# Two row tiles of a Fourier product taken by symmetry: rows turned through memory instead of multiplied

## The chip, the core and the metric

The kernel runs on one core of one Trainium2 chip. A core has five engines, each working through its own list of instructions in order: TensorE (PE, matrix products into PSUM), VectorE (DVE), ScalarE (ACT), GpSimd (POOL) and SyncE (SP, which here only issues DMAs). They wait for each other through semaphores. POOL can issue DMAs as well, and the indirect ones, whose row addresses come out of a table in SBUF, are issued there. The metric is device time in microseconds (us) of one execution; lower is better.

## The reference, cut to what matters

There are four batches of 768 positions and 8 heads of 64. First block-sparse causal attention is computed, whose heads side by side give `x`, 768 rows of 512. Then an FNet layer follows, and that is what the change touches:

```python
X = np.fft.fft(x, axis=1)               # over the 768 positions
X = np.fft.fft(X, axis=2)               # over the 512 columns
mixed = np.real(X).astype(np.float32)
u = x + mixed
mu, var = mean and variance of u over a row
un = (u - mu) / np.sqrt(var + 1e-06)
ch = np.maximum(un @ w_ch1, 0.0) @ w_ch2     # 512 -> 2048 -> 512
return (u + ch).astype(np.float32)
```

`x` is real, so the real part of its two-dimensional transform has a symmetry: row 768-k holds the same numbers as row k, with column 512-l in place of column l (indices modulo 768 and 512).

## The kernel before, in words

**One list orders all work.** `ORDER` (L114) is a long string of steps, each a short name and its indices. The loop at the end of the kernel function, under `tc.manual_schedule` (L842), calls the step's function for each, and the instructions are appended to the engines' lists in that order. No scheduler moves anything afterwards. A second string, `PLACES`, says for each PSUM tile which of four slots (`ps0` to `ps3`, two banks each) it takes. So a PE step that opens a new tile waits until the last reader of the slot's former tile is done.

**Attention** goes by pairs of heads, numbered 0 to 15, four to a batch. For pair P, `g`, `gt`, `gx`, `gl`, `gm` work out which key blocks are kept (PE, then DVE), `K` writes the mask rows (POOL, L473), `s:P,i` are the score products (PE), `e:P,i` the exponentials (ACT, `s_exp`, L516), `d:P,i` cuts the diagonal blocks (POOL, L522), `v` multiplies with the values (PE, L534), `x` divides and writes `x_b` (DVE). `kc`, `qs`, `kh`, `vc` bring keys, queries and values into place (ACT and POOL).

**The Fourier stage of batch b** folds `x` by its symmetries (`fs`, `fd`, `f` on DVE, `fc` on POOL), and multiplies over positions: `y:b,h,gg` (PE, L604) gives two PSUM tiles, h = 0 and 1, which `ty:b,h` brings to SBUF (ACT, `y_copy`, L617) and `tr:b,h` copies once more with the columns reversed (DVE, `y_turn`, L624). The second product, over columns, is `m:b,kp` (PE, `m_mm`, L636 and L637). Each call makes two of the six row tiles of 128 rows, with eight matmuls of 256 columns; the even and the odd columns of the result stand in separate halves. Row tiles 0, 1 and 2 read `ty`, row tiles 3, 4 and 5 read `tr`.

`u:b,kt` (DVE, `m_u`, L650) adds `x` to row tile kt and sums its rows, and reads the product straight from PSUM. `nm` (ACT, L658) makes the mean of it, `xu` (ACT, L664) writes the centred tile in half precision, `un` (SP, L679) is a DMA that transposes this tile into `unT`, and `bn` (DVE, L684 and L685) makes the variance.

**The two products with the weights** are `w:b,it` (PE, `w1_mm`, L719), which reads all of `unT` and makes one of 16 hidden tiles, `r` (ACT, L729, or DVE, L727) its ReLU, and `c:b,st,h` (PE, `w2_mm`, L744), which makes half of the sum over hidden tiles for row tile st: eight matmuls of 512 columns. `o` (DVE, L756) adds the result to `u`, and `od` (SP, L761) stores it. `nv` and `nr` work out the reciprocal deviation (DVE and POOL). The six `u` tiles of a batch live in three buffers of two tiles each, out of a pool of five; a buffer comes free when its `od` DMAs have landed.

The work of neighbouring batches is interleaved: while the Fourier stage of batch 3 goes its way through ACT, DVE and SP, PE works on `c` steps of batch 2.

Of the kernel before, what the change touches and what calls it, by code (L numbers as in the profile page):

```python
# [11 lines left out]
FP = mybir.dt.float32  # L12
# [7 lines left out]
S = 768  # L20
DM = 512
# [70 lines left out]
for _pieces in SC_TILES:  # L92
# [16 lines left out]
R3 = (1,)  # L109
W2_CUTS = (0, 256, 384, 512)  # L110
# [4 lines left out]
tq:0,0 qc:0,0 Lk:1 tk:0,0 ks:0,0 tk:0,1 ks:0,1 kc:0,1 tq:0,1 kh:0 kc:0,0 qc:0,1 qs:0 tk:1 ks:1 kh:1  # L115
g:0 gt:0 gx:0 gl:0,0 gl:0,1 gm:0 Lk:2 tk:2 Lq:1 tq:1 qc:1 qs:1 ks:2 kh:2 iz:0 iz:1 s:0,2 kc:1 e:0,2
s:0,5 e:0,5 g:1 gt:1 gx:1 gl:1,0 gl:1,1 gm:1 kc:2 s:0,4 e:0,4 s:0,3 s:0,0 e:0,0 e:0,3 Lq:3 Lq:2 tq:2
qc:2 qs:2 tq:3 qc:3 d:0,4 s:1,4 e:1,4 Lk:4 Lv:0 vc:0 d:0,3 d:0,2 d:0,0 d:0,5 s:0,1 e:0,1 d:0,1 g:2
gt:2 gx:2 gl:2,0 gl:2,1 gm:2 s:1,0 e:1,0 s:1,1 s:1,2 e:1,1 tk:4 ks:4 kh:4 Lk:3 tk:3 ks:3 kh:3 qs:3
d:1,4 e:1,2 d:1,2 kc:4 kc:3 v:0 x:0 s:1,3 e:1,3 d:1,3 Lq:4 tq:4 qc:4 fs:0,1 s:2,2 g:3 s:1,5 e:2,2  # L120
gt:3 gx:3 gl:3,0 gl:3,1 s:2,1 e:1,5 Lv:1 vc:1 qs:4 s:2,5 e:2,1 d:1,5 d:1,1 d:2,2 e:2,5 d:1,0 d:2,5
g:4 gt:4 s:2,0 e:2,0 gx:4 gm:3 Lk:5 tk:5 s:2,3 ks:5 s:2,4 d:2,1 kh:5 d:2,0 e:2,3 d:2,3 Lq:5 tq:5
qc:5 qs:5 gl:4,0 fs:0,0 gl:4,1 Lv:2 e:2,4 d:2,4 vc:2 kc:5 v:1 x:1 s:3,2 e:3,2 Lv:3 vc:3 s:3,4 g:5
gt:5 gx:5 gm:4 fs:1,0 gl:5,0 e:3,4 d:3,4 s:3,3 s:3,0 e:3,0 s:3,5 e:3,5 d:3,5 d:3,2 d:3,0 e:3,3 d:3,3
v:2 gl:5,1 x:2 fs:2,0 fs:2,1 gm:5 fs:1,1 fd:2,1 fd:2,0 s:3,1 e:3,1 d:3,1 W:1 s:4,1 e:4,1 s:4,2 s:4,3
e:4,3 e:4,2 v:3 x:3 fs:3,1 fs:3,0 fd:3,1 fd:3,0 f:0,1 fc:0 f:0,0 s:4,5 s:5,2 e:5,2 e:4,5 d:4,5 s:4,0
e:4,0 d:4,0 s:5,0 e:5,0 LT:0 Lq:6 Lk:6 s:5,1 tk:6 ks:6 e:5,1 d:4,2 d:5,2 d:4,3 s:4,4 e:4,4 d:5,1
y:0,0,0 y:0,0,1 ty:0,0 kc:6 f:0,2 f:0,3 y:0,1,0 y:0,1,1 ty:0,1 tr:0,0 tr:0,1 s:5,3 e:5,3 s:5,4 e:5,4
LF:0 m:0,0 u:0,0 nm:0,0,1 xu:0,0 u:0,1 nm:0,1,1 m:0,2 s:5,5 e:5,5 u:0,4 nm:0,4,1 xu:0,1 u:0,5
nm:0,5,1 m:0,1 u:0,2 u:0,3 xt:0,0 tq:6 qc:6 xt:0,1 un:0,0 W:0 Lv:4 vc:4 d:4,1 kh:6 d:4,4 d:5,0 v:4  # L130
xu:0,4 xt:0,4 nm:0,2,1 xu:0,5 xt:0,5 un:0,2 g:6 gt:6 xu:0,2 nm:0,3,1 xu:0,3 xt:0,2 xt:0,3 w:0,6,2
w:0,6,0 w:0,5,2 w:0,5,0 un:0,1 w:0,5,1 w:0,6,1 r:0,5 r:0,6 gx:6 gl:6,0 gl:6,1 gm:6 x:4 w:0,3 r:0,3
Lq:7 tq:7 Lk:8 tk:8 ks:8 fs:4,0 Lk:7 tk:7 ks:7 bn:0,0 bn:0,4 qs:6 s:6,3 e:6,3 s:6,2 s:6,4 e:6,4
s:6,1 e:6,2 e:6,1 w:0,4,2 w:0,4,1 w:0,4,0 w:0,2 r:0,4 r:0,2 kc:8 w:0,7,2 w:0,0 w:0,7,1 r:0,0 w:0,7,0
r:0,7 d:5,4 W:2 w:0,13 d:5,3 d:5,5 d:6,1 d:6,4 d:6,3 qs:7 s:6,5 e:6,5 Lv:5 s:6,0 kh:7 g:7 gt:7 gx:7
gl:7,0 gl:7,1 gm:7 e:6,0 bn:0,1 Lq:8 Lc:0 tq:8 Lq:9 w:0,14 r:0,14 r:0,13 w:0,15 w:0,12 r:0,15 kh:8
vc:5 v:5 x:5 K:7 d:6,2 qs:8 kc:7 r:0,12 s:7,2 e:7,2 d:7,2 w:0,11 r:0,11 g:8 gt:8 gx:8 gl:8,0 fs:5,1
fs:5,0 gl:8,1 gm:8 d:6,5 X:0 s:7,0 e:7,0 d:7,0 X:1 d:6,0 K:8 Lk:9 tk:9 ks:9 kh:9 tq:9 bn:0,5 bn:0,3
# [738 lines left out]
```

## Time and profile before

| | |
|---|---|
| median of 3 runs | 284.72 us (283.73 to 284.79) |
| profiled execution, its own time | 284.69 us |
| its span (first to last instruction) | 283.0 us |
| PE busy | 273.7 us, 97% of the span |
| DVE busy | 190.8 us, 67% |
| ACT busy | 166.3 us, 59% |
| POOL busy | 120.7 us, 43% |
| granted TensorE clock, mean | 0.999 |

The span is shorter than the execution's own time by 1.7 us, which lie around it. An engine's busy time is the union of its instructions' intervals. A matmul's interval in the profile is longer than the step at which the next one follows, so that a busy PE can hide gaps of about 0.1 us. For a sum, the step from one start to the next is what counts.

### The profile page before, as it was taken

How to read it: one execution, taken by the hardware profiler on the slowest of the kernel's cores; microseconds unless marked ns; L12 is line 12 of the kernel's file. 1: busy time of each engine (PE TensorE's matmuls, PEld its weight loads, DVE VectorE, ACT ScalarE, POOL GpSimd, SP SyncE). 2: the span in 40 equal slices, each digit the busy share in tenths (PEclk: the TensorE clock that was granted, in tenths of full speed). 3: DMA queues.
4: the chain of work that ended last, by engine and by line, in shares of the span. 5: the costliest groups of instructions: out<-in, count | busy, mean ns of one | idle time of the engine just before them, and what ended most of it. 6: DMA issues, size and time to landing. Idle time of an engine off the chain costs nothing.

```text
span 283.0 us, 6718 instructions
## 1 busy us (share of the span) xinstructions
PE 273.7 (97%) x2593; PEld 170.0 (60%) x2593; DVE 190.8 (67%) x570; ACT 166.3 (59%) x222; POOL 120.7 (43%) x313
## 2 busy tenths in 40 slices
PE   7799998999999999999999999999999999999995
PEld 3567676876656646565665574566576555665453
DVE  2789998998899797998988669550376443380032
ACT  3599899668787269886497634669641261343100
POOL 2157839306895658747546538701522000002000
PEclk9999999999999999999999999999999999999999
DMA  7999999996999999459795152610000042000044
GB/s 179 231 218 212 222 189 154 182 189 115 156 136 203 150 131 211 63 107 193 153 205 108 28 161 74 120 71 0 0 3 2 30 110 46 2 37 0 2 166 169
DMA packets 119152, 33.45 MB, mean 118 GB/s; under 512 B 110736, under 2 KB 115920, under 8 KB 119120
## 3 DMA queue, kind: packets, MB, share of 16 engines
q1 hardware_dynamic: 113712, 28.43, 50.7%
q0 software_dynamic: 3664, 4.19, 9.6%
q10 hardware_dynamic: 1744, 0.40, 0.7%
q8 instruction: 20, 0.33, 0.5%
q14 instruction: 12, 0.10, 0.1%
HBM read 28.55 MB, written 6.29 MB: 123 GB/s over the span
## 4 chain that ended last, share of the span: by engine, by line
PE 81%; DVE 7%; DMA 3%; ACT 3%; POOL 3%; issue 2%; ACTq 0%; POOLq 0%; DVEq 0%
PE c L744 28%; PE h L719 28%; PE sc L499 7%; PE av L534 6%; PE yp L604 3%; ACT pt L516 2%; PE mx L636 2%; DMA nat<-in_k_dram 2%; PE mx L637 2%; DMA nat<-in_q_dram 1%; PE c L737 1%; DVE kr L362 1%; PE g L424 1%; PE sc L494 1%; POOL qk L246 1%
## 5 line engine op out<-in xcount | busy, mean ns | idle before, releaser
L516 ACT ACTIVATE pt<-sc 128x1024 f16<-128x1024 f32 (+1 forms) x96 | 82.8, 926 | 25.7 <-PE sc L499 17.5
L719 PE MATMUL h<-unT,w 128*128 128x256 f16 (+1 forms) x528 | 87.2, 321 | 0.0
L744 PE MATMUL c<-w_sb,hT 128*128 128x512 f16 x368 | 83.8, 379 | 0.0
L719 PEld LDWEIGHTS <-w 128*128 128x128 f16 x528 | 50.8, 98 | 31.0 <-issue 0.3
L744 PEld LDWEIGHTS <-hT 128*128 128x128 f16 x368 | 35.6, 98 | 40.2 <-issue 0.5
L729 ACT ACTIVATE hT<-h 128x768 f16<-128x768 f32 x48 | 37.8, 811 | 34.9 <-PE h L719 34.9
L522 POOL TENSOR_SCALAR_AFFINE_SELECT pt<-pt 128x256 f16<-128x256 f16 x96 | 38.0, 421 | 35.3 <-ACT pt L516 34.8
L756 DVE SCALAR_TENSOR_TENSOR u<-c,rs,u 128x512 f32<-128x512 f32 (+2 forms) x26 | 17.6, 702 | 36.4 <-PE c L744 33.3
L727 DVE TENSOR_SCALAR hT<-h 128x768 f16<-128x768 f32 x16 | 15.1, 951 | 22.0 <-PE h L719 21.9
L246 POOL TENSOR_SCALAR_AFFINE_SELECT qk<-mt 32x160 f16<-32x160 f16 x72 | 23.6, 348 | 14.1 <-DVE mt L471 12.6
L246 POOL TENSOR_SCALAR_AFFINE_SELECT qk<-q 64x768 f16<-64x768 f32 (+1 forms) x25 | 20.8, 832 | 18.8 <-DVE q L398 7.4
L499 PE MATMUL sc<-qk 96*128 96x512 f16 (+3 forms) x144 | 26.7, 306 | 0.0
L534 PEld LDWEIGHTS <-pt 128*128 128x128 f16 x672 | 22.2, 97 | 2.3 <-issue 0.7
L534 PE MATMUL av<-v,pt 128*128 128x65 f16 x672 | 23.0, 193 | 0.3 <-POOL v L246 0.3
L243 POOL TENSOR_TENSOR t<-vr,rs 128x6 f32<-128x6 f32 x12 | 2.7, 225 | 41.0 <-DVE rs L695 40.2
L499 PEld LDWEIGHTS <-qk 96*128 96x128 f16 x144 | 12.9, 98 | 9.2 <-issue 0.8
L246 POOL TENSOR_SCALAR_AFFINE_SELECT v<-nat 128x768 f16<-128x768 f32 x16 | 14.7, 922 | 5.2 <-DMA nat<-in_v_dram 5.1
L650 DVE SCALAR_TENSOR_TENSOR u<-mx,x 128x512 f32<-128x512 f32 x24 | 15.3, 683 | 2.1 <-PE mx L637 1.9
L494 PE MATMUL sc<-qk 64*128 64x512 f16 (+3 forms) x112 | 14.8, 307 | 1.9 <-ACT pt L516 0.6
L664 ACT ACTIVATE x<-u,nm 128x512 f16<-128x512 f32 x24 | 16.1, 712 | 0.3
L684 DVE BATCH_NORM_STATS2 bst<-u 128x6 f32<-128x512 f32 x24 | 16.1, 672 | 0.0
L243 DVE TENSOR_TENSOR x<-av,rcp 128x768 f16<-128x768 f32 x16 | 15.3, 958 | 0.6
(106 smaller groups left out, 318.0 us busy)
## 6 DMA issues: line engine op xcount, KB each, us to landing
nat<-in_v_dram SPq DMA_DIRECT2D x16, 384.0 KB, 5.0
out_dram<-u SPq DMA_DIRECT2D x23, 256.0 KB, 2.5
nat<-in_k_dram SPq DMA_DIRECT2D x38, 96.0 KB, 3.7
nat<-in_q_dram SPq DMA_DIRECT2D x38, 96.0 KB, 3.8
nat<-in_k_dram SPq DMA_DIRECT2D x12, 192.0 KB, 4.5
nat<-in_q_dram SPq DMA_DIRECT2D x12, 192.0 KB, 5.1
w_sb<-in_moe_w_ch_dram POOLq DMA_DIRECT2D x2, 1024.0 KB, 11.6
w<-in_moe_w_ch_dram POOLq DMA_DIRECT2D x2, 768.0 KB, 8.1
```

What stands on the lines that cost most here:

```text
L243: (eng or nc.vector).tensor_tensor(out=out, in0=in0, in1=in1, op=op)
L246: nc.gpsimd.affine_select(out=out, in_=in_, pattern=[[0, i] for i in n], base=0, channel_multiplier=0, compare_op=ALU.is_ge, fill=0.0)
L494: nc.tensor.matmul(ps[:, e, co:co + q1 - q0], qk[hs[e], 1, XW(P), 128 * jt:128 * jt + 128], qk[hs[e], 0, XW(P), q0:q1], start=(co == 0), s ...
L499: nc.tensor.matmul(ps[:, e, co:co + q1 - q0], qk[0:96, e, 1, 128 * jt:128 * jt + 128], qk[0:96, e, 0, q0:q1], start=True, stop=True)
L516: nc.scalar.activation(out=d["pt"][:, o:o + 2 * n].rearrange("p (e c) -> p e c", e=2), in_=d["sc", i][:, :, 0:n], func=AF.Exp, scale=0.125)
L522: nc.gpsimd.affine_select(out=dg, in_=dg, pattern=[[0, 2], [1, 128]], base=0, channel_multiplier=-1, compare_op=ALU.is_ge, fill=0.0)
L534: nc.tensor.matmul(av[:, e, 66 * st:66 * st + 65], pt[:, co:co + 128], vv[:, e, jt, 0:65], start=(cnt == 0), stop=(cnt == 20))
L664: nc.scalar.activation(out=x_t[b][:, kt, :], in_=u_t[b, kp][:, k2, :], func=AF.Identity, scale=0.0625, bias=u_t[b, kp, "m"][:, k2:k2 + 1])
L719: nc.tensor.matmul(hp[:, l:r], w1s, unT[:, dt, l:r], start=(dt == 0), stop=(dt == NDT - 1))
L729: nc.scalar.activation(out=hT, in_=hp, func=AF.Relu)
L744: nc.tensor.matmul(c_ps[b, g[0]][:, st - g[0], :], h_t[b, it][:, 128 * st:128 * (st + 1)], w2_t[0][:, it, :], start=(it == 0), stop=(it == ...
L756: nc.vector.scalar_tensor_tensor(out=o, in0=ps, scalar=st_t[b][1][:, st:st + 1], in1=o, op0=ALU.mult, op1=ALU.add)
```

## The change

For the third and fourth batch (`MIRROR = (2, 3)`) the step `m:b,2`, which multiplied out row tiles 4 and 5, is gone. Their rows are 512 to 767, and by the symmetry they are rows 256 down to 1 with the columns reversed. These rows lie in row tiles 0 and 1 and in the first row of tile 2, and take another way:

- `mr:b,0` and `mr:b,1` (ACT, `m_rev`): row tiles 0 and 1, and the first row of tile 2, are copied from PSUM to an SBUF tile `rev` (in the buffer of `zw`) with the columns reversed and put back into natural order. Each call is two instructions.
- `md:b` (SP, `m_send`): two DMAs write the 257 rows, 512 KB and 2 KB, to a DRAM tile `back`.
- `ml:b` (POOL, `m_fetch`): two indirect DMAs of 256 KB each fetch the rows in reverse order into a `u` buffer. The row numbers stand in `turn`, which an `iota` on POOL writes at the start.
- `u:b,4` and `u:b,5` (DVE) now add `x` to that buffer in place, in natural column order, and read SBUF instead of PSUM.
- `tr:b,h` copies 128 reversed columns in place of 384, since only row tile 3 still reads them.

`ORDER` and `PLACES` are new as a whole. On every engine the steps stand as before until shortly after the first `w` steps of batch 0 (`w:0,4`), and in another order from there on.

```diff
+MIRROR = (2, 3)
...
+    dpool = ctx.enter_context(tc.tile_pool(name="turned", bufs=1, space=bass.MemoryType.DRAM))
...
+    turn = ctile([128, 2], mybir.dt.uint32, "turn")
...
     def y_turn(b, h):
         tr = bpool.tile([128, 2, S // 2], F16, tag=f"tr{h}", name=f"tr{h}_{b}")
-        nc.vector.tensor_copy(out=tr, in_=ys[b, h, 0][:, :, S // 2:0:-1])
+        n = 128 if b in MIRROR else S // 2
+        nc.vector.tensor_copy(out=tr[:, :, 0:n], in_=ys[b, h, 0][:, :, S // 2:S // 2 - n:-1])
         ys[b, h, 1] = tr
...
+    def m_rev(b, kp):
+        mps = m_ps[b, kp]
+        if b not in rev_t:
+            rev_t[b] = bpool.tile([128, 3, DM], FP, tag="zw", name=f"rev_{b}")
+        if kp == 0:
+            out, src = rev_t[b][:, 0:2, :], mps
+        else:
+            out, src = rev_t[b][0:1, 2:3, :], mps[0:1, 0:1, :]
+        nc.scalar.copy(out=out[:, :, 511:1:-1].rearrange("p k (m two) -> p k two m", two=2),
+                       in_=src[:, :, 1:511].rearrange("p k (two m) -> p k two m", two=2)[:, :, ::-1])
+        nc.scalar.copy(out=out[:, :, 0:2], in_=src[:, :, 0:512:511])
+
+    def m_send(b):
+        rev = rev_t[b]
+        rev_t[b, "d"] = back = dpool.tile([257, DM], FP, tag="back", name=f"back_{b}")
+        nc.sync.dma_start(back[0:256].rearrange("(k p) d -> p k d", p=128), rev[:, 0:2, :])
+        nc.sync.dma_start(back[256:257, :], rev[0:1, 2, :])
+
+    def m_fetch(b):
+        back = rev_t[b, "d"]
+        u_t[b, 2] = u_b = bpool.tile([128, 2, DM], FP, tag="u_b", name=f"u2_{b}", bufs=5)
+        for k2 in range(2):
+            nc.gpsimd.indirect_dma_start(
+                u_b[:, k2, :], None, back[:, :],
+                bass.IndirectOffsetOnAxis(ap=turn[:, k2:k2 + 1], axis=0))
+
     def m_u(b, kt):
         kp, k2 = kt // 2, kt % 2
...
+        if mps is None:
+            nc.vector.scalar_tensor_tensor(out=u_t[b, kp][:, k2, :], in0=u_t[b, kp][:, k2, :],
+                                           scalar=1.0, in1=x_b[:, kt, :], op0=ALU.mult,
+                                           op1=ALU.add, accum_out=st_t[b][2][:, kt:kt + 1])
+            return
...
+        nc.gpsimd.iota(turn, [[-128, 2]], base=256, channel_multiplier=-1)
```

The parts of the old and the new `ORDER` around the second product of batches 2 and 3:

```diff
-y:2,0,0 o:1,1 y:2,1,0 o:1,0 y:2,1,1 od:1,1 y:2,0,1 ty:2,1 c:1,4,0 ... ty:2,0 tr:2,1 ... tr:2,0 ... m:2,1
-d:12,1 d:12,0 d:13,0 m:2,0 u:2,3 u:2,2 c:1,4,1 u:2,0 nm:2,2,2 u:2,1 m:2,2 ...
+y:2,1,1 tk:14 qs:13 g:13 c:1,1,1 c:1,0,1 tk:15 gt:13 ... ty:2,0 ty:2,1 tr:2,1 tr:2,0 ks:15 gm:13
+kc:12 s:12,2 e:12,2 o:1,1 o:1,0 m:2,0 mr:2,0 s:12,1 e:12,1 od:1,1 od:1,0 m:2,1 mr:2,1 md:2 kh:14
+qs:14 vc:13 K:13 kh:15 tq:15 c:1,2,0 u:2,0 u:2,1 nm:2,0,2 s:12,5 s:12,4 e:12,5 xu:2,1 u:2,2 bn:2,2
+u:2,3 bn:2,3 e:12,4 c:1,3,0 Lv:14 s:12,3 e:12,3 s:13,3 e:13,3 xu:2,0 un:2,1 un:2,0 c:1,3,1 s:13,5
+e:13,5 s:13,1 e:13,1 s:13,2 e:13,2 c:1,4,0 nm:2,2,2 xu:2,3 un:2,3 ml:2 s:12,0 e:12,0 d:12,0 o:1,3
+u:2,4 u:2,5 nm:2,4,2 bn:2,5 xu:2,2 un:2,2 kc:14 d:12,3 d:12,5 xu:2,4 un:2,4 xu:2,5 un:2,5 qs:15
+d:12,4 d:12,1 d:13,2 c:1,5,0 g:14 gt:14 ... g:15 gt:15 bn:2,0 gm:14 c:1,5,1 s:13,0 ... w:2,2
...
-y:3,0,0 y:3,0,1 y:3,1,0 ty:3,0 y:3,1,1 c:2,0,1 tr:3,0 ty:3,1 tr:3,1 c:2,1,1 m:3,0 o:2,0 o:2,1 c:2,2,1
-u:3,0 od:2,1 od:2,0 u:3,1 m:3,2 nm:3,0,2 xu:3,0 m:3,1 u:3,4 xu:3,1 u:3,5 c:2,4,0 un:3,1 u:3,2
-nm:3,4,2 xu:3,4 u:3,3 un:3,4 c:2,3,0 bn:3,5 nm:3,2,2 xu:3,2 xu:3,5 un:3,2 xu:3,3 c:2,3,1 un:3,5
-c:2,4,1 un:3,3 un:3,0 c:2,5,0 c:2,5,1 w:3,5 ...
+y:3,1,0 y:3,0,0 f:3,3 y:3,1,1 y:3,0,1 ty:3,0 c:2,1,1 ty:3,1 m:3,0 mr:3,0 tr:3,0 tr:3,1 m:3,1 mr:3,1
+md:3 ml:3 o:2,1 od:2,1 u:3,0 u:3,1 c:2,0,1 o:2,0 od:2,0 u:3,2 u:3,3 c:2,2,0 c:2,3,0 c:2,2,1 c:2,4,0
+c:2,5,0 c:2,3,1 c:2,5,1 c:2,4,1 u:3,4 bn:3,1 nm:3,0,2 xu:3,1 xu:3,0 un:3,0 nm:3,2,2 xu:3,2 un:3,2
+xu:3,3 un:3,3 un:3,1 u:3,5 nm:3,4,2 xu:3,4 un:3,4 xu:3,5 un:3,5 w:3,9 ...
```

149 lines of the change are left out of this document (73 added, 76 removed).

## The prediction

> **What bounds the kernel now.** I read the page first, then busy time by stretches, PE's own waits, and the chain that ended last.
>
> ```profile
> PE 273.7 (97%) x2593; PEld 170.0 (60%) x2593; DVE 190.8 (67%) x570; ACT 166.3 (59%) x222; POOL 120.7 (43%) x313
> PE   7799998999999999999999999999999999999995
> 40.00:50.00 10.00, 8.59 (x105) 5.93 (x101) 9.01 (x16) 9.31 (x12) 7.03 (x16) 1.00 1.03 147
> 60.00:70.00 10.00, 10.00 (x109) 6.76 (x106) 8.66 (x19) 8.77 (x11) 4.30 (x9) 1.00 0.84 143
> 80.00:90.00 10.00, 9.71 (x133) 6.37 (x131) 9.21 (x32) 7.61 (x11) 8.23 (x20) 1.00 1.20 190
> 190.00:200.00 10.00, 10.00 (x67) 6.18 (x66) 0.66 (x1) 9.17 (x13) 1.58 (x4) 1.00 0.01 2
> 230.00:240.00 10.00, 10.00 (x51) 4.86 (x50) 2.05 (x6) 2.22 (x4) 0.00 (x0) 1.00 0.32 66
> 270.00:283.00 13.00, 9.76 (x77) 6.08 (x75) 4.67 (x8) 0.00 (x0) 0.00 (x0) 0.98 0.50 182
> PE mx L636 <- DVE tr L624: 0.7, 1, 0.7
> PE av L534 <- POOL v L246: 0.3, 1, 0.3
> ```
>
> The columns of the stretches are length, then busy time of PE, weight loads, DVE, ACT, POOL. TensorE carries the time: after 60 us its stretches are full but for 0.29 us between 80 and 90 and the 3.2 us tail. The steps stand as before up to about 65 us, so the poor stretch at 40 to 50 stays (its 0.7 us wait for `tr` is of batch 0). The rest is PE-bound. So a PE step saved counts in full if the new order still feeds PE, and every new PE wait counts in full too. The new order cannot gain over the old by feeding better: 0.3 us is all the old loses there.
>
> **The part that is certain: 16 matmuls go.** Batch 3 shows what one `m` step costs, and the pace of its neighbours.
>
> ```profile
> 219.01 2.05 ACT L617 CAST ty<-yp 128x772 f16<-128x772 f32 x2 [5.89 <-PE yp L604]
> 219.84 3.61 PE L744 MATMUL c<-w_sb,hT 128*128 128x512 f16 x16
> 223.29 0.27 PE L636 MATMUL mx<-fd_sb,ty 128*128 128x256 f16 x1
> 224.16 1.89 PE L744 MATMUL c<-w_sb,hT 128*128 128x512 f16 x8
> 227.63 10.52 PE L744 MATMUL c<-w_sb,hT 128*128 128x512 f16 x48
> 227.82 7.90 SPq L679 DMA_TRANSPOSE unT<-x  x6
> 237.99 2.33 PE L719 MATMUL h<-unT,w 128*128 128x512 f16 x13
> 201.47 3.90 PE h L719 x24
> 201.03 0.43 PE sc L499 x2
> ```
>
> From 223.29 to 224.16, 0.87 us, lies one `m` step; one goes in each of two batches: **-1.74 us**. Nothing else runs on PE in their stead. One `c` half takes (237.99-227.63)/6 = 1.73 us, one `w` step 1.30, one score tile 0.43. The shorter `tr` saves DVE time that hid under PE; counted as nothing.
>
> **Batch 3: what has to lie under `c` steps.** Let 0 be the start of `c:2,1,1`, which follows `y`. The durations besides:
>
> ```profile
> L516 ACT ACTIVATE pt<-sc 128x1024 f16<-128x1024 f32 x80 | 78.1, 1033 | 21.6 <-PE sc L499 14.1 <-PE sc L506 4.6 <-PE av L534 2.6
> L664 ACT ACTIVATE x<-u,nm 128x512 f16<-128x512 f32 x24 | 16.1, 712 | 0.3
> L658 ACT ACTIVATE nm<-sm 128x2 f32<-128x2 f32 x9 | 1.7, 202 | 14.1 <-DVE u L650 14.1
> L650 DVE SCALAR_TENSOR_TENSOR u<-mx,x 128x512 f32<-128x512 f32 x24 | 15.3, 683 | 2.1 <-PE mx L637 1.9
> L684 DVE BATCH_NORM_STATS2 bst<-u 128x6 f32<-128x512 f32 x24 | 16.1, 672 | 0.0
> L756 DVE SCALAR_TENSOR_TENSOR u<-c,rs,u 128x512 f32<-128x512 f32 x23 | 16.4, 742 | 33.3 <-PE c L744 33.3
> L810 POOL DMA_DIRECT2D w<-in_moe_w_ch_dram x3 | 2.5, 840 | 0.0
> out_dram<-u SPq DMA_DIRECT2D x23, 256.0 KB, 2.5
> unT<-x SPq DMA_TRANSPOSE x18, 2.5
> w<-in_moe_w_ch_dram POOLq DMA_DIRECT2D x1, 512.0 KB, 5.9
> ```
>
> *A new wait on PE.* Before, two `c` halves stand between `y` and `m:3,0`, and the first `ty` began a step early. Now both `ty` wait for the last `y`, one half (1.73) is the cover, and the two copies take 2.05 from about 0.2: the third matmul of `m:3,0` can start at 2.3, and two ran before it. **+0.4 us.** `m:3,0` ends at 2.95, `m:3,1` at 3.8; nine halves follow, to 3.8+15.5 = **19.4**, where `w:3,9` needs all of `unT`.
>
> *The turned copies.* `mr:3,0` moves 1020 columns a partition in its first instruction. 1024 contiguous ones take 1.03 us, the strided `ty` 1.03 for 772, or 1.37 scaled; between, 1.2, and 0.2 for the small one (`nm`): done at 4.5. `mr:3,1` (510 on one partition, by `xu` 0.7, and 0.2) at 5.4. `u:3,0` waits for `mr:3,0`: DVE loses 1.4 us there, which costs PE nothing since its next reader is far off.
>
> *SP.* Queued behind `md:3` stand `od:2,1`, `od:2,0`, then the transposes. `o:2,0` follows `u:3,0`, `u:3,1` and ends at 6.6; its DMA lands 2.5 later, at 9.1. That matters: `u:3,2` takes the buffer that this DMA frees. So `u:3,2`, `u:3,3` end at 10.4, `nm` and `xu:3,2` at 11.35, and from there SP issues five transposes, each 7.90/6 = 1.3 apart or a little less (1.25): the last is issued at 16.4 and lands at 18.9. Slack against 19.4: **0.5 us**.
>
> *The gather.* No row shows an indirect DMA. The write of 512 KB starts at 4.5 and lands after 2.5 (the 256 KB row) to 5.0 (twice that); I take 3.5, as parts of the 2.5 are fixed: 8.0. From then to the landing of both gathers: at least 0.84+2.5 = 3.3 (one issue, then a landing as for a 256 KB store), at most 0.84+5.9 = 6.7 (512 KB loaded from POOL, behind one more issue); I take 4.5, nearer the low end because the 5.9 row moved its data beside other loads: 12.5. `u:3,5`, `nm`, two `xu` (together 2.3) and the last transpose must be issued by 16.9, so the gather may land as late as 14.5. Slack **2.0**; in the worst corner it lands at 4.5+5.0+6.7 = 16.2 and PE waits 1.8.
>
> **Batch 2.** Further rows:
>
> ```profile
> L383 ACT CAST qk<-k 64x768 f16<-64x768 f32 x18 | 14.9, 829 | 0.3
> L246 POOL TENSOR_SCALAR_AFFINE_SELECT qk<-mt 32x160 f16<-32x160 f16 x72 | 23.6, 348 | 14.1 <-DVE mt L471 12.6
> L246 POOL TENSOR_SCALAR_AFFINE_SELECT qk<-q 64x768 f16<-64x768 f32 x18 | 14.9, 828 | 1.5 <-DVE q L325 0.8
> L246 POOL TENSOR_SCALAR_AFFINE_SELECT v<-nat 128x768 f16<-128x768 f32 x16 | 14.7, 922 | 5.2 <-DMA nat<-in_v_dram 5.1
> L522 POOL TENSOR_SCALAR_AFFINE_SELECT pt<-pt 128x256 f16<-128x256 f16 x96 | 38.0, 421 | 35.3 <-ACT pt L516 34.8
> L435 DVE STREAM_TRANSPOSE gt<-g 128x160 f32<-128x160 f32 x9 | 3.0, 338 | 3.2 <-PE g L424 3.2
> ```
>
> Let 0 be the start of `g:13`. PE: two halves to 3.9, `s:12,2` to 4.3, `m:2,0` to 5.2, `s:12,1`, then `m:2,1` to 6.5. ACT: the two `ty` end at 1.3, `kc:12` (two of L383) at 2.9, `e:12,2` follows its tile and ends at 5.5, `mr:2,0` at 6.9, `e:12,1` at 7.9, `mr:2,1` at 8.8. By the values taken above the write lands at 12.3. POOL has by then done `qs:14` (two of 0.83), `vc:13` (0.92) and `K:13` (eight of 0.35, 2.8), by about 8.6, and waits for it; behind stand the `d` steps of pair 12, whose first needs `e:12,0` at 18.0 anyway. The gather lands at 16.8. DVE reaches `u:2,4` at 14.0 and waits. Behind that stands `gt:14`, which frees the PSUM slot of `s:13,0`; PE, after five more halves, comes to that tile at 20.8. Before it DVE needs two `u` (1.4), `bn` (0.8) and `gt` (0.5 with its memsets), so `u:2,4` must start by 18.1. Slack **1.3**; in the worst corner (8.8+5.0+6.7 = 20.5) PE waits 2.4. On ACT the four `mr` instructions lie under PE's halves, except for about 0.2 us at `c:1,4,0`, whose slot `e:13,5` frees.
>
> **The new order elsewhere.** I followed PE against the others where a slot or a mask is taken soon after it is made. Thin joins, each with a wait of 0 to 0.3: `v:7` behind `d:7,3` (POOL does two `vc` and three `d` just before), `w:1,7` behind `e:11,4`, `s:11,3` behind `K:11`, `w:2,8` and `w:2,11` behind `r:2,5` and `r:2,8`, on an ACT without a gap. Together, with batch 2's 0.2, I take **+0.7**; bounds 0 and 3. The old order's own loss after 65 us goes: **-0.3**. The `iota` lies before POOL's first real work, in a stretch that is otherwise unchanged and where POOL waits 6.2 us in the row below; by the POOL rows above it takes under 1: nothing.
>
> ```profile
> 8.62 0.82 POOL L246 TENSOR_SCALAR_AFFINE_SELECT qk<-q 128x768 f16<-128x768 f32 x1 [6.22 <-ACT qk L373]
> 38.68 0.95 POOL L810 DMA_DIRECT2D w<-in_moe_w_ch_dram  x1
> w_sb<-in_moe_w_ch_dram POOLq DMA_DIRECT2D x2, 1024.0 KB, 11.6
> ```
>
> **The sum.** 284.69 - 1.74 + 0.4 + 0.7 - 0.3 = 283.75, **283.8 us**. The profiled execution is the median but for 0.03.
>
> **Rivals.**
> - *All joins hold* (PE waits only for `ty`, or not at all): 284.69 - 1.74 + 0.4 - 0.3, **283.0**. For it: the old order, as thin, lost 0.3. Against: 0.1 us late shows at once.
> - *The gather is late* (slower). Both slacks are used up if write and gathers together take over 8.0 + 2.0 in batch 3 and 8.0 + 1.3 in batch 2, counted from `mr`'s end. In the worst corner the waits are 1.8 and 2.4: 283.8 + 4.2 = **288.0**. It decides, that is comes out over 286.1, from about 10.8 us. Against it stands that both 5.0 and 5.9 are upper ends.
> - *The first indirect DMA is slow* (slower). If POOL must first bring in what the operation needs, only batch 2 is hit, and its slack of 1.3 goes first; from 3.6 us more than estimated the time is over 286.1. With the longest landing of any POOL DMA, 11.6 for 1 MB, it comes at 12.3+11.6 = 23.9, 5.8 past the limit: **289.6**. Against: POOL's first DMA of all, at 38.68, took 0.95 where the three average 0.84. [...]
> - *ACT is the bound from 100 to 208 us*. At 190 to 200 it is 9.17 of 10 busy. If five thin joins wait 0.5 each in place of 0.7 in all: 283.8 + 1.8 = **285.6**; if ten do, 288.
> - *The saving is not on the path*: if PE waits for `unT` in batch 3 anyway, the 0.87 there buys nothing and the wait is 0.87 longer: within the ranges above, about **284.7**.
>
> **How the numbers follow.** Forecast (283.3 to 284.7) 0.37; all joins hold 0.32; late gather or slow first one 0.13, of which 0.11 over 286.1; ACT-bound joins or a lost saving 0.18, of which 0.12 over 286.1. A change within 0.5% (283.3 to 286.1) is about what a measurement here cannot tell from none. Faster 0.32; same 0.37 + 0.02 + 0.06 = 0.45; slower 0.23. The range leaves out about 0.1 each side: 282.6 to 287.0. Since the signs mix, the forecast's own is 283.3 to 284.7.
>
> **What would show it.** In the profile after: the matmuls of `m` fall from 96 to 80; PE idles about 0.4 at `m:3,0`, for ACT's `ty`; `unT` of batch 3 lands before the last `c` half ends; `u:2,4` waits for a DMA on DVE with no PE wait behind it. I am wrong if PE waits for `unT` or `gt:14`, if the turned copy takes over 2 us, or if PE's waits after 65 us come to more than 3 us.

## The result, and the profile after

The changed kernel takes 283.35 us (median of 11 runs, 283.02 to 284.71) against 284.72 us of the kernel before (11 runs measured with it, 283.73 to 285.23). The ratio is 0.9961, with a 95% interval of 0.9946 to 0.9976. Measured again, it took 283.39 us, 0.9949 (0.9930 to 0.9968). So it is faster, by some 0.4%, which lies inside the 0.5% that the prediction called hard to tell from no change. The profiled execution took 283.30 us with a span of 281.6 us, 1.4 us less than before.

The page of the changed kernel, and its busy time by stretches (length, then PE, weight loads, DVE, ACT and POOL, then the granted clock, the DMA share and GB/s):

```profile
PE 272.2 (97%) x2577; PEld 168.8 (60%) x2577; DVE 187.5 (67%) x570; ACT 168.3 (60%) x230; POOL 122.9 (44%) x318
```

```profile
80.00:90.00 10.00, 9.63 (x136) 6.65 (x134) 6.86 (x18) 6.96 (x8) 8.76 (x21) 1.00 1.17 180
120.00:130.00 10.00, 9.88 (x114) 6.24 (x110) 9.34 (x33) 8.91 (x11) 3.46 (x11) 1.00 0.76 126
190.00:200.00 10.00, 10.00 (x65) 5.97 (x63) 1.78 (x7) 9.58 (x13) 5.89 (x19) 1.00 0.01 2
210.00:220.00 10.00, 9.93 (x71) 6.13 (x69) 5.09 (x12) 3.54 (x4) 1.54 (x4) 1.00 0.00 1
270.00:281.60 11.60, 8.59 (x60) 5.05 (x58) 3.25 (x6) 0.00 (x0) 0.00 (x0) 0.99 0.32 113
```

PE has 16 matmuls less and still does not stop: between 60 and 270 us it loses 0.37 us at 80 to 90, 0.12 at 120 to 130, 0.03 at 180 to 190 and 0.07 at 210 to 220, together 0.59, where the kernel before lost 0.29 in all. DVE gave back 3.3 us (1.2 of it the shorter `tr`), and ACT, which has the turned copies in addition, took 2.0 more; neither shows in the time.

Line numbers have moved: in the changed kernel L641 and L642 are `m`, L781 `c`, L756 `w`, L621 `ty`, L653 and L655 `mr`, L660 and L661 `md`, L667 `ml`, L687 `u` from PSUM, L683 `u` from SBUF, L716 `un`. This is the way of batch 3 in the list of instructions in order of time, first PE and then the others:

```profile
217.57 1.89 PE L781 MATMUL c<-w_sb,hT 128*128 128x512 f16 x8
...
219.41 0.27 PE L642 MATMUL mx<-fd_sb,ty 128*128 128x256 f16 x1
219.75 0.28 PE L641 MATMUL mx<-fd_sb,ty 128*128 128x256 f16 x1
...
221.29 15.70 PE L781 MATMUL c<-w_sb,hT 128*128 128x512 f16 x72
236.83 1.35 PE L756 MATMUL h<-unT,w 128*128 128x512 f16 x7
...
217.77 1.92 ACT L621 CAST ty<-yp 128x772 f16<-128x772 f32 x2 [5.18 <-PE yp L608]
220.66 1.09 ACT L653 COPY rev<-mx 128x1020 f32<-128x1020 f32 x1 [0.97 <-issue]
...
221.82 0.38 SPq L660 DMA_DIRECT2D back<-rev  x1
...
225.35 1.04 POOL L667 DMA_INDIRECT u<-back,turn  x1 [11.10 <-DMA back<-rev]
226.69 0.95 POOL L667 DMA_INDIRECT u<-back,turn  x1 [0.30 <-issue]
...
226.17 0.69 DVE L687 SCALAR_TENSOR_TENSOR u<-mx,x 128x512 f32<-128x512 f32 x1 [2.21 <-DMA out_dram<-u]
...
229.01 0.69 DVE L683 SCALAR_TENSOR_TENSOR u<-u,x 128x512 f32<-128x512 f32 x1 [1.52 <-DMA u<-back,turn]
...
224.77 10.18 SPq L716 DMA_TRANSPOSE unT<-x  x6
```

Three readings. The third matmul of `m:3,0` starts 0.34 us after the second, where the step is 0.11: **0.23 us of idle PE**. The second `ty` ended at 217.77 + 1.92 = 219.69, 0.06 us before that matmul. From the end of `m:3,1` to the first `w` step PE has nine `c` halves without a gap (72 matmuls from 221.29). And the last of the six transposes is issued at about 233.75 (224.77 + 10.18, less its own 1.2), lands about 2.4 us later at 236.2 (an estimate from the median of this line's transposes), and the first `w` matmul runs at 236.83 without a wait. Of the new DMAs, with the median from issue to landing as the last number:

```profile
back<-rev SPq DMA_DIRECT2D x2, 512.0 KB, 2.8
u<-back,turn POOLq DMA_INDIRECT x4, 3.5
```

### The profile page after: what moved, and what is told of

Its sections match the earlier page's. It is cut to its first block, busy times and chain, and to the rows that moved or that the text cites. A ratio compares the mean times of both kernels' runs of the same rounds, so it can differ in the third digit from the quotient of the medians.

```text
span 281.6 us, 6726 instructions
## 1 busy us (share of the span) xinstructions
PE 272.2 (97%) x2577; PEld 168.8 (60%) x2577; DVE 187.5 (67%) x570; ACT 168.3 (60%) x230; POOL 122.9 (44%) x318
## 5 line engine op out<-in xcount | busy, mean ns | idle before, releaser
L756 PE MATMUL h<-unT,w 128*128 128x256 f16 (+1 forms) x528 | 87.0, 321 | 0.0
L781 PE MATMUL c<-w_sb,hT 128*128 128x512 f16 x368 | 83.2, 379 | 0.0
L756 PEld LDWEIGHTS <-w 128*128 128x128 f16 x528 | 51.0, 98 | 31.3
L781 PEld LDWEIGHTS <-hT 128*128 128x128 f16 x368 | 35.7, 98 | 40.7 <-issue 0.5
L249 POOL TENSOR_SCALAR_AFFINE_SELECT qk<-mt 32x160 f16<-32x160 f16 x72 | 23.0, 340 | 10.1 <-DVE mt L475 6.9
L701 ACT ACTIVATE x<-u,nm 128x512 f16<-128x512 f32 x24 | 16.4, 714 | 0.3
L721 DVE BATCH_NORM_STATS2 bst<-u 128x6 f32<-128x512 f32 x24 | 16.2, 677 | 0.1
L687 DVE SCALAR_TENSOR_TENSOR u<-mx,x 128x512 f32<-128x512 f32 x20 | 12.8, 678 | 3.4 <-DMA out_dram<-u 2.2
L387 ACT CAST qk<-k 64x768 f16<-64x768 f32 x18 | 14.9, 828 | 0.2
```

The lines of the kernel that those rows point to most:

```text
L249: nc.gpsimd.affine_select(out=out, in_=in_, pattern=[[0, i] for i in n], base=0, channel_multiplier=0, compare_op=ALU.is_ge, fill=0.0)
L701: nc.scalar.activation(out=x_t[b][:, kt, :], in_=u_t[b, kp][:, k2, :], func=AF.Identity, scale=0.0625, bias=u_t[b, kp, "m"][:, k2:k2 + 1])
L721: nc.vector.bn_stats(out=bst, in_=u_t[b, kt // 2][:, kt % 2, :])
L756: nc.tensor.matmul(hp[:, l:r], w1s, unT[:, dt, l:r], start=(dt == 0), stop=(dt == NDT - 1))
L781: nc.tensor.matmul(c_ps[b, g[0]][:, st - g[0], :], h_t[b, it][:, 128 * st:128 * (st + 1)], w2_t[0][:, it, :], start=(it == 0), stop=(it == ...
```

## The experiments

The theory to be tested: PE is the bound from start to end, so the 16 matmuls count in full (0.87 us a batch), the gathers are hidden with little slack in batch 3 and more in batch 2, and the new order costs the few tenths that it makes PE wait. The rivals: the gain belongs to the order; the saving of batch 3 is lost to the chain of write, gather and transposes; the gathers cost nothing at any length.

### The order alone, and one batch alone

The first kernel keeps the new order (with other slots where the products stand) and computes all six row tiles by products:

```diff
-MIRROR = (2, 3)
+MIRROR = ()
-... m:2,0 mr:2,0 ... m:2,1 mr:2,1 md:2 ... c:1,2,0 u:2,0 ... ml:2
+... m:2,0 ... m:2,1 ... c:1,2,0 m:2,2 u:2,0 ...
-... m:3,0 mr:3,0 ... m:3,1 mr:3,1 md:3 ml:3 o:2,1
+... m:3,0 ... m:3,1 m:3,2 o:2,1
```

> The new order and the new places in the accumulators, but the last two row tiles of batches 2 and 3 computed by products again (no turned copy, no write, no gather). Theory: the symmetry removes 16 matmuls of 0.11 us from a TensorE that does not stop, so this kernel is 1.74 us longer than the changed one: about 285.1 us, and the new order by itself is worth nothing or costs a few tenths. Rival one: the gain came from the order and not from the symmetry: then at most 283.6 us. Rival two: half of the saving was off the path: 284.2 us. The trace should show 96 matmuls of the second product, no idle TensorE of more than 0.4 us between 70 and 260 us except at the first second product of batch 3 (0.2 to 0.3).

Measured: 285.79 us (6 runs, 285.62 to 286.49), 1.0045 of the kernel before (1.0028 to 1.0061). The rivals fall: the order by itself does not gain. In this form it costs 1.2 us, and the kernel is 0.7 us above the 285.1 that was expected. The span is 2.6 us above the changed kernel's, not 1.74. Its list of PE instructions shows where (its `c` stands at L780, `m` at L640 and L641, the scores at L502, `u` at L686):

```profile
165.26 0.28 PE L502 MATMUL sc<-qk 96*128 96x128 f16 x2
165.80 0.60 PE L502 MATMUL sc<-qk 96*128 96x512 f16 x2 [0.26 <-DVE u L686]
166.24 1.89 PE L780 MATMUL c<-w_sb,hT 128*128 128x512 f16 x8
...
219.01 1.89 PE L780 MATMUL c<-w_sb,hT 128*128 128x512 f16 x8
...
223.60 15.70 PE L780 MATMUL c<-w_sb,hT 128*128 128x512 f16 x72
```

In batch 3 the way from the one `c` half to the nine takes 223.60 - 219.01 = 4.59 us against 221.29 - 217.57 = 3.72 in the changed kernel: 0.87, as the theory has it. In batch 2 there are the same 0.87, and 0.44 more, because the scores behind `m:2,2` take a slot that DVE is still reading; that loss belongs to how this experiment puts the products back. The remaining 0.4 lie in the first 60 us (0.1) and behind the last `c` step (0.3), where both kernels have the same instructions.

The second kernel takes the products back in batch 3 alone (with other slots, and with `u:3,4` and `u:3,5` directly behind `u:3,3`):

```diff
-MIRROR = (2, 3)
+MIRROR = (2,)
-... m:3,0 mr:3,0 ... m:3,1 mr:3,1 md:3 ml:3 o:2,1
+... m:3,0 ... m:3,1 m:3,2 o:2,1
```

> As the changed kernel, but only batch 2 by symmetry; batch 3 computes its last two row tiles by products again (8 matmuls, the third product after the second). Theory: each batch is worth 0.87 us, so +0.87: about 284.2 us. Rival: in batch 3 the saving is eaten by the chain of write, gather and transposes (its transposes land only 0.65 us ahead of the first layer), so this kernel is at the time of the changed one, 283.35 us, or below.

Measured: 284.55 us (12 runs), 0.9999 of the kernel before (0.9985 to 1.0013). It is 1.2 us slower than the changed kernel, so the rival (batch 3 gives nothing) falls. Its span is 1.1 us longer, and its own list has again

```profile
217.66 1.89 PE L780 MATMUL c<-w_sb,hT 128*128 128x512 f16 x8
...
222.25 15.70 PE L780 MATMUL c<-w_sb,hT 128*128 128x512 f16 x72
```

4.59 us between the two. So 0.87 is shown. Of the other 0.2 of the span, 0.1 is there before this place and 0.1 arises behind the last `c` step, where no instruction differs.

How much of such a remainder is chance was seen when the changed kernel was run again:

> The changed kernel itself, beside the next run on the same chip: 283.35 us as before, and 0.995 to 0.997 of the kernel before.

Measured: 283.39 us (6 runs), ratio 0.9949 (0.9930 to 0.9968). In the two profiled executions of this same kernel the first `m` matmul of batch 2 stands at

```profile
160.34 0.27 PE L641 MATMUL mx<-fd_sb,ty 128*128 128x256 f16 x1
```

and, in the second one, at

```profile
160.72 0.27 PE L641 MATMUL mx<-fd_sb,ty 128*128 128x256 f16 x1
```

The difference of 0.38 us stands there already at the first `w` steps (55.9 and 56.3 us). Two spans of one profile each can be told apart to about 0.4 us, and differences between two places of one profile better: from the start of the one `c` half to the nine it is 3.72 us in both (217.96 to 221.68 in the second).

### The wait for `ty`

```diff
-y:3,1,0 y:3,0,0 f:3,3 y:3,1,1 y:3,0,1 ty:3,0 c:2,1,1
+y:3,0,0 y:3,0,1 f:3,3 y:3,1,0 y:3,1,1 ty:3,0 c:2,1,1
```

> As the changed kernel, but the first Fourier product of batch 3 computes both halves of the first output group before the second group, so that its first cast on ScalarE can start about 0.9 us earlier, ahead of the second group's. Theory: the 0.23 us that TensorE waits ahead of the second product of batch 3 are the second cast's lateness, and go: about 283.1 us, and the wait of the row L641 in batch 3 falls under 0.15 us. Rival: the casts were not what it waited for, or the wait moves to the next product: 283.35 us.

Measured: 282.95 us (6 runs, 282.72 to 283.60), ratio 0.9947 (0.9930 to 0.9963). Two slots of `PLACES` change with it. It was run once more, beside the changed kernel:

> The first Fourier product of batch 3 group by group again, beside the changed kernel on the same chip. Theory: 0.25 us under the changed kernel (the idle time ahead of its first second product of batch 3 in the trace). Rival: the 0.4 us between the two in separate calls were scatter and there is no difference.

Measured: 282.92 us (6 runs, 282.73 to 283.15), ratio 0.9937 (0.9919 to 0.9955), against 283.39 for the changed kernel on the same chip. The list of the second of these runs:

```profile
217.65 1.89 PE L780 MATMUL c<-w_sb,hT 128*128 128x512 f16 x8
...
219.49 0.27 PE L641 MATMUL mx<-fd_sb,ty 128*128 128x256 f16 x1
219.59 0.27 PE L640 MATMUL mx<-fd_sb,ty 128*128 128x256 f16 x1
...
221.12 2.10 PE L780 MATMUL c<-w_sb,hT 128*128 128x512 f16 x9
```

The step at that place is 0.10 in place of 0.34, and from the one half to the nine it is 3.47 us in place of 3.72: 0.25 us gone, and nothing late behind it. This is the fastest kernel of the study, 0.5 to 0.6% below the one before. The medians differ by 0.4 to 0.5; the 0.2 beyond the shown 0.25 are within what the front stretch does by chance.

### How near the gathers are: batch 3

Three kernels delay the rows of tiles 4 and 5 and see when PE starts to wait. First both gathers of batch 3 twice, the second pair behind the landing of the first:

```diff
-        for k2 in range(2):
+        for k2 in (0, 1, 0, 1) if b == 3 else (0, 1):
             nc.gpsimd.indirect_dma_start(
```

> As the changed kernel, but the two gathers of batch 3 are issued twice, the second pair into the same rows after the first pair has landed, so that the rows arrive about 4 to 5 us later. Theory: the transposes of batch 3 land only about 0.65 us before the first layer needs them, so TensorE waits 3.5 to 4.5 us at the first layer of batch 3: about 287.3 us, and the idle time stands before the first matmul of line L756 of batch 3. Rival: the chain has more slack than the trace seems to show, or the scheduler's order hides it: under 284.5 us.

Measured: 288.8 us (5 runs, 287.12 to 292.40), ratio 1.0154 (1.0129 to 1.0178). PE's waits (total, times, longest), SP's transposes and PE's list show the expected 4 us, and the busy time of PE by stretches shows something that was not expected (the third number from the right is the granted clock):

```profile
PE h L755 <- DMA unT<-x: 4.0, 1, 4.0
226.75 15.15 SPq L715 DMA_TRANSPOSE unT<-x  x6
```

```profile
243.19 21.08 PE L755 MATMUL h<-unT,w 128*128 128x256 f16 x111 [3.99 <-DMA unT<-x]
```

```profile
240.00:243.00 3.00, 0.00 (x0) 0.89 0.43 87
243.00:245.00 2.00, 1.81 (x6) 0.50 1.00 374
245.00:248.00 3.00, 3.00 (x11) 0.50 0.04 13
248.00:250.00 2.00, 2.00 (x10) 0.71 0.00 0
250.00:252.00 2.00, 2.00 (x14) 1.00 0.00 0
```

The granted clock is 0.50 from about 242.3 us, still inside the wait, to about 249.2: 6.8 us, of which some 6 lie behind the wait (it ends at 243.19). At half the clock these would cost 3 us, an estimate from the length and the clock. The runs spread accordingly: 287.12 us at a mean clock of 1.0, 288.44 and 288.80 at 0.994, 289.77 at 0.987, 2.65 us above the first. So a mean clock can be read as a length: by arithmetic 3.4 us at 0.50 in a span of 286 us make 0.994, and 6.8 us make 0.988. The profiled execution is the longest, 292.40 us; some 1.9 us of it stand already at the first `w` steps (57.9 us in place of 55.9), in a stretch that the edit does not touch, and are not explained.

A shorter delay, one transpose twice:

```diff
-xu:3,4 un:3,4
+xu:3,4 un:3,4 un:3,4
```

> As the changed kernel, but the last transpose but one of batch 3 is issued twice into the same place, so that the last one is issued later by one or by two transposes (1.2 us of issue, 2.45 us to landing where the second waits for the first). Theory: the last transpose lands about 0.9 us before the first layer of batch 3 needs it, so TensorE waits 0.3 us if the second does not wait for the first (283.7 us), and 1.6 to 2.7 us if it does (285 to 286 us), and the granted clock stays at 1.0. Rival: a wait of this length costs the clock as the wait of 4 us did: over 287 us.

Measured: 284.80 us (10 runs), ratio 1.0019 (0.9999 to 1.0038), with a clock of 0.998 to 1.0 in every run. PE's wait, and the transposes in SP's list:

```profile
PE h L755 <- DMA unT<-x: 1.4, 1, 1.4
```

```profile
224.52 12.60 SPq L715 DMA_TRANSPOSE unT<-x  x7
```

The time is the changed kernel's 283.35 plus the wait of 1.4. The transposes take 2.4 us longer than the 10.18 of six, so the slack of the last transpose is 2.4 - 1.4 = 1.0 us. The pair of gathers gives the same: the last transpose 15.15 - 10.18 = 5.0 us later, 4.0 us of wait.

A delay in between, only the second gather twice:

```diff
-        for k2 in range(2):
+        for k2 in (0, 1, 1) if b == 3 else (0, 1):
```

> As the changed kernel, but only the second of the two gathers of batch 3 is issued twice, so that the last rows arrive about 3.5 us later (a whole pair twice made it 5.0, with 4.0 us of idle TensorE and the granted clock at 0.5 for some 6 us behind it; one transpose twice made 1.4 us of idle TensorE and no loss of clock). Theory: TensorE waits 3.5 less the 1.0 us of slack, 2.5 us, at the first layer of batch 3, and the clock stays: 285.9 us. Rival: a wait of 2.5 us already costs the clock: 287.5 to 289 us in most executions.

Measured: 286.97 us (4 runs), ratio 1.0089 (1.0058 to 1.0120). The wait is as expected,

```profile
PE h L755 <- DMA unT<-x: 2.6, 1, 2.6
```

but both answers came true. Two runs took 286.19 and 286.28 us at clocks of 1.0 and 0.998, which is 283.35 + 2.6 and a little. The other two took 287.67 and 287.84 at 0.994: 1.5 us more. So a wait of 2.6 us cost the clock in two runs of four. These two were not profiled; that the loss stands behind this wait is read from the mean clock, which is that of 3.4 us at 0.50.

### How near the gathers are: batch 2

```diff
-        for k2 in range(2):
+        for k2 in (0, 1, 0, 1) if b == 2 else (0, 1):
```

> As the changed kernel, but the two gathers of batch 2 are issued twice, the second pair after the first has landed, so that the rows arrive 4.5 to 5.0 us later (that is what the same edit did to batch 3). Theory: in batch 2 VectorE reaches the work that TensorE waits for (the copies of the counts, gt) about 3 us before it is needed, so about 1.5 to 2.0 us of the delay come out as idle TensorE between 165 and 182 us: 285.0 us. Rival one: the attention work of the next batch hides all of it: 283.4 us. Rival two: what is queued behind the gathers on GpSimd and behind the additions on VectorE makes it more than the delay: over 288 us.

Measured: 285.04 us (10 runs, 284.86 to 285.73), ratio 1.0020 (1.0001 to 1.0039): 1.7 us over the changed kernel, as expected. PE's waits name both places:

```profile
PE sc L502 <- DVE gt L438: 1.1, 1, 1.1
PE h L755 <- DMA unT<-x: 0.5, 1, 0.5
```

The same work of batch 2 in VectorE's list of the changed kernel, for comparison:

```profile
171.26 0.69 DVE L683 SCALAR_TENSOR_TENSOR u<-u,x 128x512 f32<-128x512 f32 x1 [0.56 <-DMA u<-back,turn]
...
174.66 0.35 DVE L439 STREAM_TRANSPOSE gt<-g 128x160 f32<-128x160 f32 x1 [1.75 <-PE g L428]
```

There DVE waits 0.56 us for the second gather and then 1.75 us for PE, so that PE waits for nothing. With the gathers doubled, the second addition starts at 175.58 in place of 171.26, 4.3 us later; the 1.1 is the wait that the prediction described (DVE's `gt:14` behind the additions); the 0.5, for the last transposes of batch 2, was not foreseen.

### Batch 1 as well: three that failed

If a batch is worth 0.87 us, batch 1 should be worth as much. Its step `m:1,2` goes, and `mr`, `md` and `ml` come in. All three kernels of this section also have the new order of `y` from the section on `ty`, so the time to compare with is 282.95 us.

```diff
-MIRROR = (2, 3)
+MIRROR = (1, 2, 3)
-m:1,1 u:1,3 ... u:1,1 u:1,0 ... od:0,2 ... gl:10,1 gm:10 K:10 ... od:0,3 ... m:1,2 u:1,4
+m:1,1 mr:1,1 u:1,3 ... u:1,1 u:1,0 mr:1,0 ... od:0,2 ... gl:10,1 od:0,3 md:1 ml:1 gm:10 K:10 ... u:1,4
```

> The first Fourier product of batch 3 group by group as in the run before it that did this, and batch 1 by symmetry as well: its third second-product step is gone, its two turned copies, its write and its two gathers are put in. Theory: another 8 matmuls of 0.11 us go from a TensorE that does not stop, 0.87 us below the 282.95 us of that run: 282.1 us; the gathers land at about 117 to 118.3 us, where the additions that use them run now (118.29). Rival: ScalarE's copies (1.9 us more) and the GpSimd queue, which waits for the write, hold up the masks or the transposes of batch 1, whose last lands 0.4 us ahead of the first layer: 282.9 to 284.5 us.

Measured: 292.27 us (6 runs), ratio 1.0279 (1.0251 to 1.0306). PE stood still for 5.1 us and the clock went down. The gathers were issued only at 116.8 and landed at about 122.7, and `xu` with the exponentials behind it stood on ACT's queue. That looked like the cause, so the next kernel brought them forward:

```diff
-s:8,5 e:8,5 s:9,2 ... s:9,5 m:1,0 ... xu:1,2 u:1,1 u:1,0 mr:1,0 ... od:0,2 Lk:12 ... od:0,3 md:1 ml:1
+s:8,5 m:1,0 e:8,5 mr:1,0 u:1,1 u:1,0 ... s:9,2 ... s:9,5 ... xu:1,2 ... od:0,2 md:1 Lk:12 ... od:0,3 ml:1
```

> Batch 1 by symmetry as in the run before, with its first second-product step moved up by about 4 us (ahead of the scores that stood before it), so that the turned copy, the write and the gathers run earlier; the first Fourier product of batch 3 group by group. Theory: what failed in the run before was the late landing (122.7 us in place of 118.3) behind which ScalarE's exponentials stood; with the gathers landed by about 118.5 us TensorE does not stop and the 8 matmuls count: 0.87 below 282.95, so 282.1 us. Rival: ScalarE's two more copies, or VectorE's order, stop TensorE by more than the 0.87 us: 283 to 286 us; if the gathers land after 120 us, over 286 us again.

Measured: 292.60 us (6 runs, 289.80 to 294.49), ratio 1.0284 (1.0242 to 1.0327). A third one also put an exponential ahead of the casts:

```diff
-nm:1,4,2 xu:1,4 un:1,4 xu:1,5 un:1,5 s:10,0 d:9,5 v:9 x:9 e:10,0
+s:10,0 d:9,5 v:9 x:9 e:10,0 nm:1,4,2 xu:1,4 un:1,4 xu:1,5 un:1,5
```

> As the run before it in this call, but one exponential of the attention (the first of tile 10) stands ahead of the casts of the gathered rows on ScalarE's queue, so that a late landing does not hold up the scores behind it. Theory: 282.1 us as that one if the gathers are in time, and under 284 us even if they are 2 us late. Rival: the casts come 0.4 us later and TensorE waits for the last transpose of batch 1 by as much: 282.5 us; or the wait is elsewhere: 283 to 286 us.

Measured: 291.42 us (6 runs), ratio 1.0246 (1.0217 to 1.0276), with the same wait on PE. The theory was wrong in all three. The late landing was only half of the cause. In the second kernel the gathers began 1.9 us earlier and landed at about 120.8, and its rival (landed after 120 us, over 286 us) is what happened; but in the third kernel an exponential ahead of ACT's casts did not help. What the landing holds up is POOL. The second kernel's list of POOL instructions, PE's row behind it and the stretch with its clock:

```profile
116.26 0.99 POOL L666 DMA_INDIRECT u<-back,turn  x1 [0.30 <-issue]
117.30 0.75 POOL L248 TENSOR_SCALAR_AFFINE_SELECT qk<-mt 32x160 f16<-32x160 f16 x2
120.84 2.45 POOL L248 TENSOR_SCALAR_AFFINE_SELECT qk<-mt 32x160 f16<-32x160 f16 x6 [2.80 <-DMA u<-back,turn]
...
123.05 1.01 PE L502 MATMUL sc<-qk 96*128 96x512 f16 x2 [4.03 <-POOL qk L248]
```

```profile
120.00:130.00 10.00, 6.34 (x96) 0.66 0.52 93
```

POOL does two of the eight mask copies of `K:10`, then waits 2.80 us, until the second gather has landed, and only then does the other six, on which the scores of tile 10 wait. The first kernel has the same wait, and there too PE goes on 0.24 us before the six copies end, though the profile names ACT, which finishes its casts at that moment:

```profile
122.84 2.45 POOL L248 TENSOR_SCALAR_AFFINE_SELECT qk<-mt 32x160 f16<-32x160 f16 x6 [2.97 <-DMA u<-back,turn]
...
125.05 1.01 PE L502 MATMUL sc<-qk 96*128 96x512 f16 x2 [5.05 <-ACT x L700]
```

In both kernels POOL's idle time stands between the second and the third of eight like copies, and the profile names the landing of the gathers as what ended it: 2.97 and 2.80 us. The copies read and write other tiles (`qk` from `mt`) than the gathers (`u` from `back`); why they wait for the landing no run shows. Behind the gathers of batch 2 the changed kernel shows no such wait. POOL's list there:

```profile
167.91 0.98 POOL L667 DMA_INDIRECT u<-back,turn  x1 [0.30 <-issue]
173.66 1.12 POOL L526 TENSOR_SCALAR_AFFINE_SELECT pt<-pt 128x256 f16<-128x256 f16 x3 [4.76 <-ACT pt L520]
174.74 1.71 POOL L249 TENSOR_SCALAR_AFFINE_SELECT qk<-q 64x768 f16<-64x768 f32 x2
```

The next work waits 4.76 us for ACT, and the gathers had landed by 171.3. Around the end of the 4.0 us of wait the clock is 0.66 in the mean over the ten us from 120 to 130, as much as 6.8 us at 0.50 make. For the second kernel's profiled execution an estimate comes out: 4.0 us of wait and 3.4 for 6.8 us at half clock, less the 0.87 saved, are 6.5 of the 6.85 us that its 289.80 lies above 282.95. So batch 1 loses because POOL has mask copies to make right behind its gathers, and this wait of 4 us went with a loss of clock as well (a mean of 0.982 to 0.988 in the six runs). No kernel here takes the wait away, so that part rests on the traces. A place for `ml:1` that avoids it would be some 3.5 us earlier, so that the gathers land before the copies begin at 117.3; in the second kernel the write had landed by about 110.1 (an estimate: issued at 106.15, and 3.9 from issue to landing, the median of this kernel's three writes), but other work of POOL stood ahead of the gathers. Whether that can be had stays open.

## Why the prediction was right

It named 283.8 us as the likeliest, within 283.3 to 284.7; 283.35 was measured. That is close to the lower end, and about as far from 283.75 as from the 283.0 of the rival in which all joins hold, so the time alone does not decide between them. The terms do: the saving came in full, and the waits were there but smaller than taken.

- **16 matmuls, -1.74.** Right, and in full: 0.87 for each batch, shown by the experiments in batch 3 as 4.59 against 3.72 us between the same two places.
- **The wait for both `ty`, +0.4.** It is there, at the place named, and is 0.23 us long; the `ty` copies took 1.92 in place of 2.05. Putting the first group first takes it away.
- **Thin joins, +0.7, and the old order's own loss, -0.3.** Net +0.4 was predicted. Between the first `w` steps (55.78 before, 55.91 after) and the end of the last `c` step (279.76 and 278.59) the changed kernel is 1.30 us shorter. That is 1.74 less the 0.23 of `ty` and less another 0.2, so the term was too large by about 0.2. The remaining 0.1 of the 1.4 us by which the spans differ is 0.1 lost up to the first `w` steps and 0.2 gained behind the last `c` step, within the chance of one execution. The rival of ACT as the bound between 100 and 208 us fell: ACT is 9.58 of 10 busy at 190 to 200, and yet PE loses 0.12 us between 100 and 130 and 0.03 in the 78 us from 130 on:

```profile
130.00:208.00 78.00, 77.97 (x698) 1.00 0.50 107
```

- **The chain of batch 3.** With 0 at the start of the `c` half: `mr:3,0` done at 4.2 (predicted 4.5), the first gather issued at 7.8 (8.0), the last transpose issued at 16.2 (16.4), the nine halves done at 19.3 (19.4). DVE waits 1.2 us for `mr:3,0` (1.4 predicted) and 2.2 for the buffer that `od:2,0` frees. The slack of the last transpose is 1.0 us, measured by delay, where 0.5 was worked out. Part of the difference is that one matmul of `w` runs before the wait in the delayed kernels. The gathers had less room than predicted, though: when the second one landed 3.9 us later, PE waited 2.6, and at 5.2 us later 4.0, so their slack was about 1.2 us where 2.0 was worked out.
- **The new DMAs.** The write of 512 KB landed after 2.8 us (3.5 taken, 2.5 to 5.0 bounds; the 256 KB stores beside it took 2.6 in the median), but POOL began the first gather 0.7 us later, 3.5 after the issue of the write. From the landing of the write to that of both gathers it took 5.9 us in batch 3 (0.7, then 1.3 to the second issue, then 3.8), against 4.5. The first gather of all took POOL 1.10 us where the others took 0.95 to 1.04, so the rival of a slow first one falls.
- **Batch 2.** The gather was hidden, with more room than the predicted 1.3 us: a delay of 4.3 us cost 1.7. One reason is a step of the working. It let the write start at 8.8, behind `mr:2,1`, but the 512 KB need only `mr:2,0`. With 0 at the start of `g:13` (156.03) the write was issued at 6.7 and the first gather at 10.5, where 12.3 was worked out; only `u:2,5` waited for a gather, 0.56 us.

```profile
162.68 0.38 SPq L660 DMA_DIRECT2D back<-rev  x1
```

- **The rival of a late gather** had the mechanism right: what exceeds the slack comes out as a wait of PE (2.6 and 4.0 us at 3.9 and 5.2 us later). It took a wait as its own length. That held for 1.4 us and not always for 2.6. Its own waits, 1.8 and 2.4 us, lie between, and no run shows their price. (The 1.8 is 1.7 by its own figures, 16.2 less 14.5.)
- **What the prediction did not see** is the wait of POOL for the gathers in the instructions behind them, 2.97 and 2.80 us in batch 1. It asked what POOL does before the gathers and which `d` steps come after; it did not ask whether the next copies wait for the landing. Here nothing hung on it.

## What to carry to other kernels

Work taken from TensorE, which hardly stopped here, counted in full (0.87 us a batch in batches 2 and 3), but only where the replacement landed in time (with batch 1 the medians were 8.5 to 9.7 us longer), and that margin is best measured by doubling a transfer and reading the wait that comes out. Ask of a DMA that an engine issues not only what it waits for, but what stands behind it on that engine and whether that waits for the landing, as POOL's copies did for 2.80 and 2.97 us. And price an idle TensorE by more than its length: 1.4 us cost only itself here, but 2.6 us was paid again in clock in two of four runs.

## What the hardware showed beyond what was expected

- **The clock after a wait.** Idle TensorE of 1.4 us: a mean clock of 0.998 to 1.0 in all ten runs. 2.6 us: a mean clock of 0.994 in two of four runs and 1.5 us more. 4.0 us before the first layer of batch 3: 0.987 to 0.994 in four of five runs and 1.0 in the fifth. The stretch at a clock of 0.50 was 6.8 us long in that kernel's profiled execution. In those of the first two kernels with batch 1 (waits of 5.1 and 4.0) a mean clock of 0.66 from 120 to 130 us makes the same 6.8 us at 0.50, and in that of the third (4.0) 0.83 makes 3.4 us. It began inside the wait where the stretches are fine enough to show it: at 242.3 us in the wait from 239.2 to 243.2 in batch 3, and at 122.8 in the one from 120.0 to 125.05 of the first kernel with batch 1. In the stretch at half clock the rows by shape of the kernel with both gathers twice read

```profile
L755 PE MATMUL h<-unT,w 128*128 128x512 f16 x9 | 5.7, 634 | 0.0
```

  634 ns for a matmul of 512 columns, which takes 379 at full clock (the mean of this line in the changed kernel). How long TensorE must stand still to lose clock, the runs do not settle: 1.4 us did it in none of ten runs, 2.6 us in two of four runs, and 4.0 us before the first layer of batch 3 not in every run.
- **An indirect DMA of 256 KB in 128 rows** held POOL for 0.95 to 1.10 us, with 0.30 us between two of them, and landed 3.3 to 3.8 us after its issue in the changed kernel. In batch 1 it took about 4.5 us: in the first kernel DVE could go on at 121.30 and 122.75 behind gathers begun at 116.81 and 118.20, in the second at 120.75 behind the one begun at 116.26. The write of 512 KB before it landed after 2.8 to 2.9 us in the changed kernel, and after 3.9 in the median of the three writes of the second kernel with batch 1.
